# A gated-MLP stage in nine chunks of 512 tokens, with matmul operands set apart in SBUF

## The chip, the cores and the metric

The kernel runs on one core of a Trainium2 chip. The metric is device time in microseconds (us) for one execution. The kernel before takes 1077.67 us, the median of three runs (1074.98, 1077.67, 1080.53). A core has a matmul engine (TensorE, PE in the profile; its weight loads are PEld), VectorE (DVE), ScalarE (ACT), GpSimd (POOL) and SyncE (SP), which here issues nearly all DMAs. Each engine runs its own queue in order. Data lies in SBUF, 128 partitions wide; a "word" below is 4 bytes of one partition, and "columns" is the free size of a matmul's moving operand.

## The reference

Attention with positive random features, then a gated MLP over the 4608 tokens:

```python
def phi(x):                       # x scaled by D**-0.25
    h = x @ omega.T - sum(x*x)/2
    return exp(h - max(h)) / sqrt(128)
kv  = einsum('bhsm,bhsd->bhmd', phi(k), v)
z   = phi(k).sum(axis=2)
num = einsum('bhsm,bhmd->bhsd', phi(q), kv)
den = einsum('bhsm,bhm->bhs', phi(q), z)[..., None] + 1e-06
x   = (num / den) as (4608 tokens, 512)          # 8 batches x 576 tokens, 8 heads x 64
out = (sigmoid(x @ w_gate) * (x @ w_val)) @ w_out   # 512 -> 1536 -> 512
```

All arithmetic is float32. The matmuls of the MLP are made of parts: an operand a is split into a high part (rounded to fp32r, the type that TensorE takes at full speed) and a low part a - high, and a product is the sum of three matmuls, low x high, high x low and high x high.

## The kernel before, in words

**Stage 1** (to 457.77 us) computes the attention and, between its matmuls, the gate and value products of the first NE = 4 of the 12 column tiles of the hidden layer (`products`, L534, output `gv`), in chunks of 512 tokens of which the first is two of 256. Its order comes from a planner, `Turns`, that simulates the engines with costs written in the code. The attention's output goes to DRAM as `xT`, and stage 1's gated values as `ye`. From 390.65 us on only the products are left. At the end of stage 1 `first_operands` loads and divides the operands of stage 2's first chunk, and `early_unit` (L459) loads and divides the first UL = 5 weight units that `late_weights` had stored in `w32`. A unit is the seven sums and blocks of a weight matrix that Strassen's scheme wants, in a high and a low part.

**Stage 2** (`second_pass` L692, `gated` L618, matmuls at L634, output `gw`) does the other 8 column tiles, as four pairs of tiles, with Winograd's form of Strassen's 2 x 2 scheme: seven products instead of eight. Tokens go in NCW = 6 chunks of 768; the two halves of a chunk (W = 384 tokens) are one dimension of the 2 x 2 scheme, so a matmul has 384 columns. In each chunk a loop runs over the four pairs, and for each over kind 0 (gate) and kind 1 (value): eight groups, n = 0 to 7. A group has 7 products of 6 matmuls: 42. A group's matmuls and its evacuations on ACT, DVE and POOL stand in an order written by hand (`pin` keeps it): products 1, 6, 5, then the previous group's last two (4, 3; "held", so 12 matmuls of a group run within the next one), then 2 and 7. Between them `between` runs the work that a plan names for (chunk, group, place): loading and dividing the next chunk's operands (`operands`, L585), in chunk 0 the division of the UE = 3 units that stage 1 has not divided (twelve steps, three to a group from group 1), and in the last chunk the first loads of stage 3 (`first_values`, L767). DVE adds the products up from PSUM (`add`, L616); after kind 1 POOL does seven steps for the pair, and the seven combinations that stage 3 wants go to DRAM as `yl`, in two parts, `ya` (4 of 7) and `yb` (3 of 7). `put` (L687) issues these stores on SP, at the next group of kind 1.

The stage-2 operands xh and xl (high and low part of one of seven combinations) lie in one buffer of a ring of 8 (`buffer`, L435): XL = 7 in the pool `late`, XE = 1 in the pool `tail`. Each is [2, 2, W] words, 6144 bytes in a partition. Six more units, those of the output weights, come into the units' places in the last chunk (`unit`, L440; the DMA is L445): one after each of the groups 1 to 5, the last behind the loop.

**Stage 3** (`last(g)`, L787, matmuls at L810, output `po`) goes over 18 groups of 2 x 128 tokens. For each of six slices j it takes the seven combinations (`gated_values`, L731: for j below 2 from `ye`, with four sums at L752, else from `yl`), divides them into yh and yl (`parts_of`, L754: ACT at L760, then DVE or POOL at L762) and runs 21 matmuls of 256 columns; here yh or yl is the loaded weight, and the unit is the moving operand. yh and yl lie in the same ring of buffers, at an offset in words: APART = 80, but where PLACED names (g, j) its pair of offsets. The values of the groups' slices j >= 2 lie in one tile for a group: group 0's tile takes a unit's place. After slice 0 of group 0, the loads of group 1 are issued; after slice 1, the last stores of stage 2.

The places in SBUF follow from the pools: `const` has a pad, `below`, of 80 words. In the kernel before, stage 2's units and operand buffers all begin at the same place modulo 512 bytes.

## Time and the profile before

| | |
|---|---|
| median of three runs | 1077.67 us |
| the profiled execution | 1078.5 us |
| its span | 1076.7 us |
| instructions | 26339 |
| TensorE matmul busy | 1050.9 us, 98%, 10556 |
| DVE, ACT, POOL busy | 758.3, 491.5, 404.3 us |
| DMA moved | 226.32 MB |
| stage 2's matmuls (L634) | 2016 of 384 columns, 334 ns each |
| stage 3's matmuls (L810) | 2268 of 256 columns, 280 ns each |

The span is the time from the first to the last instruction in the trace. The ns of a matmul is its own duration; matmuls are pipelined and overlap, so the distance from one start to the next, the pace, is shorter, and the share of busy time says little. What sets the time is read from the chain of waits (what each step waited for, followed back from the end) and from counts in windows.

### The profile page before, as it was taken

The page shows a single profiled execution, that of the slowest core. Times are in us where ns is not written, and L with a number is a line of the kernel's source. Part 1 is how long each engine was busy: PE and PEld are TensorE (multiplying, and loading weights), DVE is VectorE, ACT ScalarE, POOL GpSimd, SP SyncE. Part 2 cuts the span into 40 slices and gives each one's busy share as a digit, 9 for nine tenths or more (in the row PEclk, how much of TensorE's full clock was granted, in tenths as well). Part 3 has the DMA queues.
Part 4 walks back from the last instruction along what each step waited for, and adds up shares of the span by engine and source line. Part 5 has one row for each costly group of instructions (what it writes and reads, how often), then busy time and mean ns, then how long its engine had stood idle before and what let it go on. Part 6 is the DMA issues. An engine that isn't in the chain of part 4 may idle for free.

```text
span 1076.7 us, 26339 instructions
## 1 busy us (share of the span) xinstructions
PE 1050.9 (98%) x10556; PEld 979.2 (91%) x10556; DVE 758.3 (70%) x1482; ACT 491.5 (46%) x1026; POOL 404.3 (38%) x326
## 2 busy tenths in 40 slices
PE   6789999999999999999999999999999999999998
PEld 5678888878788888899999999999999999999998
DVE  3999989999889954457747574756658666666663
ACT  6687676675555554333323232323223444443342
POOL 0331513432524323026756676656544111111111
PEclk9889999999999999999999999999999999999999
DMA  7587979898886666152423324242798765555661
GB/s 283 182 288 245 311 273 376 254 371 282 276 272 234 233 241 240 49 213 78 146 103 132 133 78 165 74 162 103 245 397 287 238 213 185 194 188 202 206 216 40
DMA packets 121322, 226.32 MB, mean 210 GB/s; under 512 B 10992, under 2 KB 59888, under 8 KB 118128
## 3 DMA queue, kind: packets, MB, share of 16 engines
q1 hardware_dynamic: 115872, 215.39, 57.8%
q10 hardware_dynamic: 5328, 9.24, 2.3%
q8 instruction: 83, 1.36, 0.5%
q14 instruction: 39, 0.32, 0.1%
HBM read 144.90 MB, written 79.69 MB: 209 GB/s over the span
## 4 chain that ended last, share of the span: by engine, by line
PE 94%; DMA 2%; DVE 2%; ACT 1%; issue 0%; SPq 0%; DVEq 0%; ACTq 0%
PE gw L634 33%; PE po L810 24%; PE gv L534 18%; PE ppq L932 4%; PE ppk L932 3%; PE pnq L1079 3%; PE pkv L1014 3%; PE ptq L1062 3%; PE pxq L1104 2%; DMA xT<-xsq 1%; ACT kpk L990 1%; DMA c8r<-w 0%; DMA rawk<-kT 0%; DVE sqq L879 0%; DMA natq<-qn 0%
## 5 line engine op out<-in xcount | busy, mean ns | idle before, releaser
L634 PE MATMUL gw<-xl,u 128*128 128x384 f32 x2016 | 350.5, 334 | 0.0
L634 PEld LDWEIGHTS gw<-xl,u 128*128 128x128 f32 x2016 | 349.2, 188 | 1.0 <-issue 0.9
L810 PE MATMUL po<-u,yh 128*128 128x256 f32 x1512 | 264.3, 280 | 0.0
L810 PEld LDWEIGHTS po<-u,yh 128*128 128x128 f32 x1512 | 230.0, 188 | 0.0
L810 PE MATMUL po<-u,yl 128*128 128x256 f32 x756 | 211.5, 280 | 0.0
L534 PE MATMUL gv<-xe,wh 128*128 128x512 f32 (+1 forms) x640 | 189.7, 376 | 0.0
L760 ACT ACTIVATE yh<-yr 128x896 fp32r<-128x896 f32 x108 | 102.5, 954 | 152.3 <-PE po L810 67.6
L762 DVE TENSOR_TENSOR yl<-yr,yh 128x896 fp32r<-128x896 f32 x91 | 102.4, 1129 | 63.3 <-ACT yh L760 62.9
L810 PEld LDWEIGHTS po<-u,yl 128*128 128x128 f32 x756 | 143.8, 190 | 0.2 <-DVE yl L762 0.2
L534 PEld LDWEIGHTS gv<-xe,wh 128*128 128x128 f32 x640 | 115.3, 189 | 19.5 <-issue 0.5
L534 PE MATMUL gv<-xe,wl 128*128 128x512 f32 (+1 forms) x320 | 120.7, 377 | 0.0
L762 POOL TENSOR_TENSOR yl<-yr,yh 128x896 fp32r<-128x896 f32 x17 | 37.0, 2177 | 208.9 <-ACT yh L760 184.0
L616 DVE TENSOR_TENSOR u<-gw,p 128x384 f32<-128x384 f32 x96 | 53.3, 555 | 67.1 <-PE gw L634 45.8
L683 POOL TENSOR_TENSOR ya<-ya,g 128x384 f32<-128x384 f32 x48 | 59.9, 1249 | 96.5 <-issue 36.7
L642 ACT ACTIVATE g<-g 128x384 f32<-128x384 f32 x72 | 37.8, 526 | 108.9 <-DVE g L616 108.8
L510 POOL TENSOR_TENSOR xe<-xr,xe 128x512 fp32r<-128x512 f32 (+1 forms) x40 | 49.5, 1261 | 80.1 <-ACT xe L501 80.1
L990 ACT ACTIVATE kpk<-ppk,nbk 128x128 f32<-128x128 f32 x256 | 70.9, 393 | 8.3 <-DVE nbk L948 8.2
L534 PEld LDWEIGHTS gv<-xe,wl 128*128 128x128 f32 x320 | 60.6, 189 | 9.9 <-PE pxq L1104 0.4
L939 DVE TENSOR_REDUCE sqk<-ppk 128x8 f32<-128x1024 f32 (+1 forms) x48 | 45.1, 953 | 20.9 <-PE ppk L932 20.7
L1067 ACT ACTIVATE qpq<-ptq 128x512 f32<-128x512 f32 (+1 forms) x80 | 42.1, 563 | 36.4 <-PE ptq L1062 36.1
L939 DVE TENSOR_REDUCE sqq<-ppq 128x8 f32<-128x1024 f32 (+1 forms) x48 | 45.5, 955 | 11.2 <-PE ppq L932 10.9
L752 DVE TENSOR_TENSOR yr<-yr 128x128 f32<-128x128 f32 x144 | 40.1, 322 | 18.7 <-DMA yr<-ye 18.2
(227 smaller groups left out, 1560.5 us busy)
## 6 DMA issues: line engine op xcount, KB each, us to landing
yr<-yl SPq DMA_DIRECT2D x72, 448.0 KB, 5.1
yl<-ya SPq DMA_DIRECT2D x24, 768.0 KB, 3.5
yl<-yb SPq DMA_DIRECT2D x24, 576.0 KB, 4.4
u<-w_parts SPq DMA_DIRECT2D x6, 1792.0 KB, 10.7
v<-va SPq DMA_DIRECT2D x32, 330.0 KB, 5.5
out<-o ACTq DMA_DIRECT2D x34, 256.0 KB, 5.5
natq<-qn SPq DMA_DIRECT2D x32, 256.0 KB, 5.5
xT<-xsq SPq DMA_DIRECT2D x64, 128.0 KB, 2.9
```

What stands on the lines that cost most here:

```text
L510: nc.gpsimd.tensor_tensor(out=x[:, 1], in0=raw[:, k], in1=x[:, 0].bitcast(F32), op=ALU.subtract)
L534: nc.tensor.matmul(gv, lhsT=u[:, s], rhs=v, start=(m == 0), stop=(m == 3 * KC - 1))
L616: return nc.vector.tensor_tensor(out=o, in0=a, in1=b, op=ALU.add)
L634: nc.tensor.matmul(o, lhsT=u[:, k, s], rhs=v[:, kc, :], start=(first and m == 0), stop=(m == 5), skip_group_check=not first,)
L683: pin(nc.gpsimd.tensor_tensor(out=o, in0=a, in1=b, op=op))
L760: pin(nc.scalar.activation(out=yh, in_=x, func=AF.Copy))
L762: pin(engine.tensor_tensor(out=yl_, in0=x, in1=yh.bitcast(F32), op=ALU.subtract))
L810: nc.tensor.matmul(o, lhsT=u[:, i, :], rhs=v[:, k, :], start=(j + m == 0 and n in (1, 6, 5, 3)), stop=(j == NPAIR - 1 and m == 2), skip_gr ...
L932: nc.tensor.matmul(pp[r, h, k, :], lhsT=raw[HALVES[h], o + r.start : o + r.stop], rhs=om_sb[HALVES[h], :], start=True, stop=True,)
L939: nc.vector.tensor_reduce(out=z[:, :, :, 0], in_=pp, axis=AX.X, op=ALU.max)
L990: nc.scalar.activation(out=kp[t][:, h, :], in_=pp[:, h, i, :], func=AF.Exp, bias=nb[:, h, i : i + 1],)
L1067: nc.scalar.activation(out=qp, in_=pt, func=AF.Exp)
```

## The change

- W is 2 x 128, so stage 2 has NCW = 9 chunks of 512 tokens, matmuls of 256 columns, 72 groups; `yl`, the stores and all tiles of a chunk shrink with it.
- The ring of operand buffers has 10 places (7 in `late`, 3 in `tail`) of ROOM = 1152 words (4608 bytes). Pads of 80 words (above the operands in `late`) and 48 words (below them in `tail`) are allocated. In stage 2 the two parts stand at words 0 and 512 of the buffer, but for operands 0, 4, 3 of chunks 1 and 4 (MIXED) at 624 and 96.
- In stage 3 the offset APART is 32, and PLACED is (48, 64) for slices (0, 1), (1, 0), (4, 0) and (10, 0).
- Stage 1 divides six units (UL = 6), the sixth behind the last chunk's inputs; stage 2's chunk 0 divides two (eight steps).
- The plan for the next chunk's operands spreads over the groups 2 to 7 and has nothing left in the next chunk's group 0.
- All six late units go into `late`'s places, after the groups 1 to 6 of the last chunk.
- Group 0's values in stage 3 get a tile of their own ("yr").

```diff
-W = 3 * P
+W = 2 * P
...
-XL, XE = 7, 1
-UL, UE = 5, 3
-PLACED = {(0, 1): (0, 48), (2, 0): (0, 48), (4, 0): (80, 0), (6, 0): (96, 112), (8, 0): (12, 10), (10, 0): (0, 48)}
-BELOW, APART = 80, 80
+XL, XE = 7, 3
+UL, UE = 6, 2
+BELOW, ABOVE_X, BELOW_X = 80, 80, 48
+ROOM, APART = 1152, 32
+MIXED = {(c, n) for c in (1, 4) for n in (0, 4, 3)}
+PLACED = dict.fromkeys(((0, 1), (1, 0), (4, 0), (10, 0)), (48, 64))
...
     def buffer(name):
         at, n = (late, XL) if turn_of[0] % (XL + XE) < XL else (tail, XE)
         turn_of[0] += 1
-        return at.tile([P, 2, 2, W], F32R, tag="x", bufs=n, name=name)
+        if turn_of[0] == XL + 1:
+            tail.tile([P, BELOW_X], F32, name="below_x")
+        return at.tile([P, ROOM], F32R, tag="x", bufs=n, name=name)
+
+    def operand(c, n):
+        b = buffer(f"xl{c}_{n}")
+        return [b[:, o : o + 2 * W].rearrange("p (k t) -> p k t", k=2) for o in ((624, 96) if (c, n) in MIXED else (0, 2 * W))]
...
     def early_unit(n):
         t = yield from after(stored[n], 0)
+        if n == UL - 1:
+            t = yield from after(x_ready[-2][-1], t)
...
     def high(x, n, a, c):
-        b = buffer(f"xl{c}_{n}")
-        x[n] = b[:, 0], b[:, 1]
-        pin(nc.scalar.activation(out=b[:, 0], in_=a, func=AF.Copy))
+        x[n] = operand(c, n)
+        pin(nc.scalar.activation(out=x[n][0], in_=a, func=AF.Copy))
...
             (c - 1, 2, 2): [combined(s, a21, a22, ALU.add)],
-            (c - 1, 3, 2): [combined(a21, a11, a21, ALU.subtract)],
-            (c - 1, 4, 2): [parts(0, a11, nc.gpsimd)],
-            (c - 1, 5, 2): [combined(a11, s, a11, ALU.subtract)],
-            (c - 1, 7, 0): [parts(4, a11, nc.vector)],
-            (c - 1, 7, 1): [parts(3, s, nc.gpsimd)],
-            (c - 1, 7, 2): [
-                parts(1, a12, nc.vector), parts(5, a21, nc.gpsimd), combined(a12, a12, a11, ALU.subtract),
-            ],
-            (c, 0, 1): [parts(2, a22, nc.vector), parts(6, a12, nc.vector)],
+            (c - 1, 3, 0): [combined(a21, a11, a21, ALU.subtract)],
+            (c - 1, 3, 2): [parts(0, a11, nc.gpsimd)],
+            (c - 1, 4, 0): [combined(a11, s, a11, ALU.subtract)],
+            (c - 1, 4, 2): [parts(1, a12, nc.vector)],
+            (c - 1, 5, 1): [parts(4, a11, nc.vector)],
+            (c - 1, 6, 0): [combined(a12, a12, a11, ALU.subtract)],
+            (c - 1, 7, 0): [parts(3, s, nc.gpsimd)],
+            (c - 1, 7, 1): [parts(2, a22, nc.vector)],
+            (c - 1, 7, 2): [parts(6, a12, nc.vector), parts(5, a21, nc.gpsimd)],
...
-                    if c == NCW - 1 and 1 <= n <= UL:
+                    if c == NCW - 1 and 1 <= n <= NPAIR:
                         unit(late, UL + UE + n - 1)
-            if c == NCW - 1:
-                unit(tail, N_LATE - 1)
...
             if len(groups) == g:
+                t, n = ("u", UE) if g else ("yr", 1)
                 groups.append(
-                    tail.tile([P, NPAIR - EP, N_OPS, P], F32, tag="u", bufs=UE, name=f"yr{g}") if g < 2 else groups[g - 2]
+                    tail.tile([P, NPAIR - EP, N_OPS, P], F32, tag=t, bufs=n, name=f"yr{g}") if g < 2 else groups[g - 2]
                 )
...
-            buffer(f"{t}{g}_{j}").rearrange("p a b t -> p (a b t)")[:, at : at + N_OPS * P].rearrange("p (o t) -> p o t", t=P)
+            buffer(f"{t}{g}_{j}")[:, at : at + N_OPS * P].rearrange("p (o t) -> p o t", t=P)
...
                 for n in (0, 4, 3, 1, 5, 2, 6):
-                    b = buffer(f"xl0_{n}")
-                    x[n] = b[:, 0], b[:, 1]
+                    x[n] = operand(0, n)
+                late.tile([P, ABOVE_X], F32, name="above_x")
```

## The prediction

> **What bounds the kernel now.** I read the page first, then the chain of waits, then windows of the matmul lines, then the queues around the change from stage 2 to stage 3.
>
> ```profile
> span 1076.7 us, 26339 instructions
> PE 1050.9 (98%) x10556; PEld 979.2 (91%) x10556; DVE 758.3 (70%) x1482; ACT 491.5 (46%) x1026; POOL 404.3 (38%) x326
> ...
> 390.65 67.12 PE gv L534 x296
> 457.77 348.09 PE gw L634 x2004
> 805.86 2.48 PE po L810 x21
> 808.34 2.08 PE gw L634 x12
> 810.42 260.57 PE po L810 x2235
> ```
>
> TensorE is busy for 98% of the span, and from 390.65 the chain is TensorE alone. So a time is a number of matmuls by a pace (start to start), plus the places where TensorE waits. Stage 2 (L634) takes 348.09 + 2.08 = 350.17 us, stage 3 (L810) 2.48 + 260.57 = 263.05 us. The profiled execution took 1078.5 us: the span and 1.8 us around it. The median of the three runs is 0.8 us lower, so I sum against 1078.5 and take 0.8 off.
>
> Paces come from windows: a window holds the matmuls that touch it, so the pace is the window plus one matmul's duration over the count. A row has the window and its length, then busy time and (count) of TensorE and of its weight loads, the granted clock, the DMA engines' busy share and their GB/s; the first two rows are of the costliest groups and end in the mean ns of one.
>
> ```profile
> L634 PE MATMUL gw<-xl,u 128*128 128x384 f32 x2016 | 350.5, 334 | 0.0
> L810 PE MATMUL po<-u,yh 128*128 128x256 f32 x1512 | 264.3, 280 | 0.0
> ...
> 470.00:740.00 270.00, 270.00 (x1556) 269.31 (x1556) 1.00 0.34 121
> ...
> 838.00:895.00 57.00, 57.00 (x487) 57.00 (x486) 1.00 0.62 204
> 896.20:898.60 2.40, 2.40 (x23) 2.40 (x22) 1.00 0.93 311
> 926.00:953.00 27.00, 27.00 (x240) 27.00 (x239) 1.00 0.61 205
> 970.00:1060.00 90.00, 90.00 (x767) 90.00 (x766) 1.00 0.54 183
> ...
> 120.20:123.40 3.20, 3.20 (x29) 3.20 (x28) 1.00 1.04 383
> ```
>
> The fourth line is the 384-wide matmul of stage 2: (270.00 + 0.334)/1556 = 173.7 ns, the whole stage at one pace. The next four are the 256-wide matmul of stage 3, which has **two paces**: (57.00 + 0.28)/487 = 117.6 and (90.00 + 0.28)/767 = 117.7 ns in the first and last, (27.00 + 0.28)/240 = 113.7 ns in the third. The granted clock is 1.00 in all of them, so it is not the clock. The kernel spreads stage 3's operands by an offset per group and slice (PLACED, APART): each change of pace that I found stands at a PLACED entry, and the pace then stays. The 2.40 us window is the block of (6, 0), with offsets 96 and 112; it runs at (2.40 + 0.28)/23 = 116.5 ns, and behind it the groups are fast. The last line is a 256-wide matmul of stage 1, whose buffers all begin at the same place modulo 512 bytes as its weights: (3.20 + 0.28)/29 = 120.0 ns. Same shape, three paces: the operands' places look like the cause. I take 113.5 ns for the fast pace (113.7, less half a matmul's edge of the count) and 117.7 for the slow one.
>
> **The change part by part.** *Stage 2's matmuls.* They go from 2016 of 384 columns to 9 x 8 x 42 = 3024 of 256. By the diff's sizes I place the new buffers: the pads of 80 and 48 words put the stage-2 operands at 80 words modulo 128 from their weights, and the MIXED ones at 96 and 112; in stage 3 the smaller APART of 32 on a base of 48 gives 80 again, and (48, 64) gives 96 and 112. So both stages have stage 3's usual distance and, at marked blocks, the mixture that came before its fast groups. Chunk 0, with no mixture ahead of it, I take as slow: 336 x 117.7 ns = 39.55 us. Chunks 1 and 4 hold three mixed operands: 144 x 116.5 + 192 x 113.5 ns = 38.57 us each. The other six: 6 x 336 x 113.5 ns = 228.8 us. The sum is 345.5 us against 350.17: **-4.7 us**. The fast pace has never been seen with L634, so this is the least certain term; its bounds are all slow, 3024 x 117.7 ns = 355.9 (+5.7), or 120.0 ns, 362.9 (+12.7), above and all fast, 343.2 (-7.0), below. I stay near the fast end because the distances are those of stage 3.
>
> The Trainium skill ("TensorE: Matmul & The Clock Gate", section "Back-to-back issue gap") gives N/2.4 + 2.5 ns for an isolated warm matmul. That is 109.2 ns at 256 and 162.5 at 384, so by it the stage would become 3024 x 109.2 - 2016 x 162.5 ns = 2.6 us longer: a price per matmul that speaks against narrower ones. The trace has 173.7 ns at 384, 11 ns over the rule, and 113.7 at 256, 4.5 over it; so the rule's price is not this kernel's, and I give it no chance of its own.
>
> *Stage 3's matmuls.* Their number stays: 18 x 126 = 2268. The mixture at (0, 1), (1, 0), (4, 0) and (10, 0) should keep all of it fast: 84 x 116.5 + 2184 x 113.5 ns = 257.7 us against 263.05: **-5.4 us** (-5.6 to +3.9, the latter for 117.7 throughout).
>
> *Loads at the change of stage.* Six 1792 KB units are loaded within the last chunk, which shrinks from 336 x 173.7 ns = 58.4 us to 38.1.
>
> ```profile
> 766.50:819.80 53.30, 53.30 (x345) 53.30 (x344) 34.29 (x51) 13.72 (x23) 31.19 (x27) 1.00 0.99 371
> 780.00:787.00 7.00, 7.00 (x43) 7.00 (x42) 2.88 (x6) 1.40 (x3) 3.65 (x4) 1.00 1.04 434
> ...
> 760.01 0.36 SPq L690 DMA_DIRECT2D yl<-ya  x1
> ...
> 761.57 4.82 SPq L745 DMA_DIRECT2D yr<-ye  x6
> 766.49 1.55 SPq L445 DMA_DIRECT2D u<-w_parts  x2
> ...
> 796.53 1.76 SPq L747 DMA_DIRECT2D yr<-yl  x4
> ...
> 803.81 0.33 SPq L445 DMA_DIRECT2D u<-w_parts  x1
> 804.23 5.49 SPq L745 DMA_DIRECT2D yr<-ye  x6
> ...
> 817.47 3.25 DVE L752 TENSOR_TENSOR yr<-yr 128x128 f32<-128x128 f32 x7
> ...
> yl<-ya SPq DMA_DIRECT2D x24, 768.0 KB, 3.5
> yl<-yb SPq DMA_DIRECT2D x24, 576.0 KB, 4.4
> u<-w_parts SPq DMA_DIRECT2D x6, 1792.0 KB, 10.7
> yr<-yl SPq DMA_DIRECT2D x72, 448.0 KB, 5.1
> ...
> L760 ACT ACTIVATE yh<-yr 128x896 fp32r<-128x896 f32 x108 | 102.5, 954 | 152.3 <-PE po L810 67.6
> L762 DVE TENSOR_TENSOR yl<-yr,yh 128x896 fp32r<-128x896 f32 x91 | 102.4, 1129 | 63.3 <-ACT yh L760 62.9
> L752 DVE TENSOR_TENSOR yr<-yr 128x128 f32<-128x128 f32 x144 | 40.1, 322 | 18.7 <-DMA yr<-ye 18.2
> ...
> PEld po L810 <- DVE yl L762: 0.2, 1, 0.2
> ```
>
> The first two rows are windows again, with DVE, ACT and POOL ahead of the last three columns; then come timelines (start, length, what was issued or run, its count) and DMA issues (KB each). From the first unit's issue at 766.49 the DMA engines are 99% busy, at 371 GB/s (434 in the best 7 us), until 819.80. Behind the six units, on the same queue, come group 1's first values (issue at 804.23), and TensorE met its first block of them just in time: 0.2 us. Bytes from the first unit's issue to those values, each row's KB by 1024: six units 11.0 MB, three pairs' stores 4.1, group 0's other values 1.8, group 1's first slice (4 blocks of 128 x 128 values, 256 KB) 0.3, together 17.2 MB, or 46.4 us: 812.9. Four sums, an ACT copy and a subtraction follow; the sums began at 817.47, 4.5 us behind that estimate, with TensorE due at 810.42 + 105 x 0.114 = 822.4. After the change the stores are 896 KB a pair, and it is 15.9 MB, or 42.7 us (36.6 at 434 GB/s). Before, the last pair's store came 12.5 us into the chunk, which starts at 457.77 + 1668 x 0.1737 = 747.5, and the unit 6.5 us later. The store goes with the chunk's length, 12.5 x 38.1/58.4 = 8.2; the issues behind it keep their 6.5. So the values land at 8.2 + 6.5 + 42.7 = 57.4 us after the chunk's start, and TensorE could use them 4 x 0.322 + 0.954 + 1.129 = 3.4 us later, at 60.8. It is due at 38.1 + 12 x 0.1135 + 126 x 0.1135 = 53.8. That is a wait of **+7.0 us**, which did not exist before: 0.8 at 434 GB/s, 11.5 with the 4.5 us that the estimate was early. I take the middle, the rate of the whole stretch. That the sixth unit's load is now in the loop and yr0 has a place of its own takes a wait off SP, but the bytes ahead of group 1 stay, so neither gains here.
>
> *Division, seams, the rest.*
>
> ```profile
> L616 DVE TENSOR_TENSOR u<-gw,p 128x384 f32<-128x384 f32 x96 | 53.3, 555 | 67.1 <-PE gw L634 45.8
> L616 DVE TENSOR_TENSOR u2o<-po,p1o 128x256 f32<-128x256 f32 x18 | 7.5, 419 | 8.8 <-PE po L810 8.8
> L454 DVE TENSOR_TENSOR u<-u 128x512 fp32r<-128x512 f32 x9 | 7.3, 814 | 2.7 <-ACT u L453 2.7
> L683 POOL TENSOR_TENSOR ya<-ya,g 128x384 f32<-128x384 f32 x48 | 59.9, 1249 | 96.5 <-issue 36.7
> L407 POOL TENSOR_TENSOR c7r<-c,c7r 128x256 f32<-128x256 f32 x2 | 1.5, 738 | 0.1
> ...
>   issue: 0.9, 5
> ```
>
> An evacuation on DVE falls from 555 to 419 ns, but there are 72 groups instead of 48. A group lasts 42 x 0.1135 = 4.77 us and has 5.5 of them, 2.3 us: free, as now. In chunk 0 eight halved units are divided at three to a group: 3 x 0.814 + 5.5 x 0.419 = 4.75 us of DVE in 4.77. That has no slack, so I charge **+1.0 us**, between 0 and 3.6 (three groups late by one division and one evacuation, 1.2 each). POOL's seven steps a pair go from about 7 x 1.2 = 8.4 us to about 7 x 0.74 = 5.2, in a pair of 9.5 us: free. TensorE had 0.9 us of hiccups at five chunk changes; eight make 1.4: **+0.5 us** (0 to 2, should DVE be short there). The sixth unit divided in stage 1 waits on SP for the last chunk's inputs and adds two ACT and two DVE steps beside 67 us of dense matmuls: nothing.
>
> **Sum:** -4.7 - 5.4 + 7.0 + 1.0 + 0.5 = -1.6, so 1076.9 us for a profiled execution and **1076.1 us** for the median.
>
> **The rivals.** *B, the loads come in time.* If DMA holds its best rate through the seam and DVE keeps up, no term but the two paces is left: 1077.7 - 10.1 = 1067.6 us. For it: 434 GB/s is in the trace, and fewer bytes of stores compete. Against: the mean over 53 us is 371, with the same transfers.
>
> *C, the mixture does not hold.* The pace could fall back at a second mixture: (2, 0) and (10, 0) in the present stage 3 turned fast groups slow, though with other offsets. With chunks 5 to 8 and six groups of stage 3 slow: 4 x 336 x 4.2 ns = 5.6 us and 6 x 126 x 4.2 ns = 3.2 us more, and 1.2 us less wait as the last chunk is longer: 1083.7 us.
>
> *D, slower: the pace never turns fast.* The mechanism is a fixed price per matmul, at place or by the way the weights come in, that no pad removes, or the change not giving the distances that I worked out. All of both stages at 117.7 ns: stage 2 +5.7, stage 3 +3.9, the wait 5.3 (TensorE is due later), 1.5 for the rest: 1077.7 + 16.4 = 1094.1 us; with stage 2 at 120.0 ns some 6 us more. It decides from the point at which stage 2's mean pace passes 115.8 ns (350.17/3024). For it: 384 columns need 173.7 ns, 0.452 a column, and 0.452 x 256 = 115.8 leaves nothing for a fixed part, while the 256-wide matmuls of the stage-1 window and of two thirds of stage 3 run at 117.6 or more. Against: 27 us at 113.7 directly behind the very mixture that is now used.
>
> The Trainium skill ("TensorE: Matmul & The Clock Gate", section "Step-by-step: what each phase is for") says that weights and moving operand have read ports of their own and a weight load takes nothing from the running matmul. By it a distance between the two buffers would buy nothing, and D would follow. The trace disagrees so far as it goes: one instruction on one shape at 113.7 and at 117.7 ns.
>
> **How the numbers follow.** Forecast 0.45, B 0.28, C 0.13, D 0.14. A measurement of this kernel can tell about 0.5%, 5.4 us, from no change: 1072.3 and 1083.1 are the bounds. The forecast's own range is 1069.9 (wait of 0.8) to 1083.2 (wait 11.5, division 3.6): 0.14 of it faster, 0.28 the same, 0.03 slower. B is faster. C lies at the upper bound, 0.06 the same and 0.07 slower; D is slower. Together 0.42, 0.34, 0.24. The range reaches from 1066, B with a little to spare, to 1085, C with the same, and leaves out D and the tails.
>
> **What would show it.** Count L634 in a window of chunks 5 to 8: 113 to 114 ns right, 117 or more C or D; the same for L810 in groups 12 to 17. In the chain, a gap ahead of L810 about 15 us into stage 3, released by L762 or L760, which in turn waited for values from ye; none there is B. On SP, the first w_parts issue should stand 14 to 16 us into the last chunk. DVE waits in groups 1 to 3 of chunk 0 should show the division. I am wrong outright if TensorE waits by more than 3 us in chunks 1 to 7, or if the pace changes at blocks that are not marked.

## The result, and the profile after

The changed kernel takes 1093.84 us, the median of four runs (1093.35 to 1094.26), beside 1078.32 for the kernel before in the same session: a ratio of 1.0144, 95% interval 1.0125 to 1.0164. It is slower by 1.4%. The forecast was 1076.1 us, with a range up to 1085.

First the page of the profile after, and its chain of waits (start, length, what it was spent on, count):

```profile
span 1091.6 us, 28952 instructions
PE 1049.0 (96%) x11564; PEld 974.7 (89%) x11564; DVE 780.6 (72%) x1636; ACT 498.7 (46%) x1117; POOL 407.6 (37%) x419
...
813.38 11.90 DMA yr<-ye
...
831.45 108.89 PE po L819 x943
...
944.07 2.11 POOL yl L771
946.23 12.21 PE po L819 x105
960.30 2.33 DVE yl L771
963.86 2.11 DMA yr<-ye
...
971.62 1.09 DVE o L626 x3
974.64 2.13 POOL yl L771
```

TensorE is busy for 1.9 us less than before, but the span is 14.9 us longer. The chain before was TensorE alone from 390.65 us on; now it leaves TensorE around the change of stage (mostly for DMA, 781 to 831) and from 941 on again and again, for DVE, the loads of first values, the evacuations with their stores, and POOL.

The windows of the two matmul lines (columns as in the prediction):

```profile
500.00:539.00 39.00, 39.00 (x339) 39.00 (x338) 1.00 0.34 121
579.00:606.00 27.00, 27.00 (x241) 27.00 (x240) 1.00 0.41 142
607.60:616.00 8.40, 8.40 (x74) 8.40 (x73) 1.00 0.27 96
655.00:769.00 114.00, 114.00 (x1008) 114.00 (x1008) 1.00 0.35 124
...
861.00:918.00 57.00, 57.00 (x504) 57.00 (x504) 1.00 0.56 194
1010.00:1086.00 76.00, 72.43 (x628) 71.44 (x627) 1.00 0.46 160
```

Stage 2 runs at (39.00 + 0.28)/339 = 115.9 ns in chunk 1, which holds mixed operands, and at (114.00 + 0.28)/1008 = 113.4 in chunks 5 to 7; stage 3 at 113.7 in groups 2 to 5. The second and third rows are chunk 3, where nothing is marked: (27.00 + 0.28)/241 = 113.2 ns up to 606 us, (8.40 + 0.28)/74 = 117.3 behind 607.6. In the last row a window of 76 us holds 628 matmuls, 121.5 ns each: there TensorE waits.

From the starts of all matmuls in the two traces I made the sums below: the time at the pace, and as waits what a distance from start to start has above the pace, where it is over 135 ns (200 at 384 columns).

| us | before | after |
|---|---|---|
| first matmul of stage 2 to the last of stage 3 | 614.5 | 629.5 |
| of it at the pace | 613.7 | 603.7 |
| waits in chunk 0 | 0.05 | 4.3 |
| waits in the chunks between | 0.5 | 0.4 |
| waits from the last chunk's start to group 2 | 0.3 | 10.8 |
| waits in groups 2 to 7 | 0.0 | 0.0 |
| waits in groups 8 to 17 | 0.0 | 10.3 |

So the paces gave 10.0 us, as forecast (about 4 in stage 2 and 6 in stage 3), and three waits took 25.

**The waits of groups 8 to 17.** The lists of what matmuls and weight loads of L819 waited for say who ends them (both engines count, so a wait stands here nearly twice):

```profile
  POOL yl L771: 15.4, 18
```

All of it lies in groups 8 to 17; DVE's yl, next in the list, is named for 1.3 us there. POOL makes yl of a group's last slice only. Why is it late? These rows of four timelines, put in order of time, are one turn of it, around the start of group 8 at 933.3 (a row joins neighbouring instructions; in brackets the idle time before and what ended it):

```profile
927.31 4.49 ACT L769 ACTIVATE yh<-yr 128x896 fp32r<-128x896 f32 x5 [7.35 <-DVE yl L771]
928.40 2.13 POOL L771 TENSOR_TENSOR yl<-yr,yh 128x896 fp32r<-128x896 f32 x1 [13.19 <-ACT yh L769]
929.14 3.34 DVE L771 TENSOR_TENSOR yl<-yr,yh 128x896 fp32r<-128x896 f32 x2 [2.26 <-ACT yh L769]
931.50 3.40 SPq L754 DMA_DIRECT2D yr<-ye  x6
931.71 0.36 ACT L835 ACTIVATE p1o<-po 128x256 f32<-128x256 f32 x1
933.28 0.95 ACT L769 ACTIVATE yh<-yr 128x896 fp32r<-128x896 f32 x1 [1.21 <-issue]
934.85 0.70 DVE L761 TENSOR_TENSOR yr<-yr 128x128 f32<-128x128 f32 x3 [2.37 <-DMA yr<-ye]
...
938.71 0.42 DVE L626 TENSOR_TENSOR u2o<-po,p1o 128x256 f32<-128x256 f32 x1
...
941.14 1.72 ACTq L846 DMA_DIRECT2D out<-o  x2
942.99 4.32 ACT L769 ACTIVATE yh<-yr 128x896 fp32r<-128x896 f32 x5 [8.76 <-DMA out<-o]
944.07 2.10 POOL L771 TENSOR_TENSOR yl<-yr,yh 128x896 fp32r<-128x896 f32 x1 [13.55 <-ACT yh L769]
```

ACT makes five yh in a row: the last slice of group 7 and four of group 8. DVE makes two yl from them; the first of them frees a place for first values, and only then SP issues the loads of group 9's (931.50). DVE's next instructions are group 9's sums, which wait for those loads (2.37 us), and the evacuation of group 7 stands behind them: it begins at 938.71, 5.4 us after the group's last matmul. ACT's next instructions are a copy out of PSUM (931.71), one more yh (933.28) and the stores of that evacuation; the yh of group 8's last slice stands behind the stores: 942.99, 15.68 us after the one of group 7. POOL needs 2.1 us for its yl, and TensorE, which reached that slice at 933.3 + 105 x 0.1133 = 945.2, starts it at 946.23. The loop ACT, DVE, SP, DVE, ACT takes about 15.5 us a group; TensorE's 126 matmuls take 14.28.

In the kernel before, around the start of its group 9 at 939.2 (fast there too):

```profile
937.75 0.70 DVE L752 TENSOR_TENSOR yr<-yr 128x128 f32<-128x128 f32 x3 [1.22 <-DMA yr<-ye]
...
939.36 0.42 DVE L616 TENSOR_TENSOR u2o<-po,p1o 128x256 f32<-128x256 f32 x1
...
941.93 0.82 ACTq L837 DMA_DIRECT2D out<-o  x2
942.88 2.04 ACT L760 ACTIVATE yh<-yr 128x896 fp32r<-128x896 f32 x2 [2.66 <-DVE o L616]
...
945.05 2.12 POOL L762 TENSOR_TENSOR yl<-yr,yh 128x896 fp32r<-128x896 f32 x1 [12.17 <-DVE yl L762]
```

The evacuation begins 0.1 us after the group's last matmul, as only a part of the sums stands ahead of it, and POOL ends at 947.2, 4 us before TensorE comes to the last slice. Stage 3 is not pinned behind group 0: its order on ACT and DVE is generated when the kernel is built, from the places that are free. In both kernels ACT has five yh between a group's stores and its next copy out of PSUM. But with ten places instead of eight they run one slice further ahead: the yh of a group's last slice, which POOL needs, is the first of the five instead of the second (POOL starts behind it, at 944.07 and 945.05). On DVE, all eight sums of group 9 now stand ahead of the evacuation of group 7; in the kernel before, some sums stand between the evacuation's steps.

**The waits at the change of stage.**

```profile
781.00:826.00 45.00, 42.22 (x352) 41.83 (x351) 23.83 (x47) 12.07 (x24) 17.61 (x24) 0.96 0.97 369
...
785.73 0.37 SPq L700 DMA_DIRECT2D yl<-yb  x1
...
797.82 0.74 POOL L693 TENSOR_TENSOR yb<-g,ya 128x256 f32<-128x256 f32 x1 [6.50 <-DMA yl<-yb]
799.27 0.42 DVE L626 TENSOR_TENSOR g<-gw,p 128x256 f32<-128x256 f32 x1 [5.09 <-POOL yb L693]
...
813.38 9.52 SPq L754 DMA_DIRECT2D yr<-ye  x6
...
827.47 2.34 DVE L761 TENSOR_TENSOR yr<-yr 128x128 f32<-128x128 f32 x7
```

The DMA engines are 97% busy for 45 us, at 369 GB/s. A store of yb, issued at 785.73 behind two units, keeps its one place until 797.8: POOL waits 6.50 us for it, DVE 5.09 us for POOL, and TensorE 2.4 us at 801 (by the starts of the matmuls). POOL waits in the same way at 808.6, 4.58 us. Group 1's first values, issued from 813.38 on, land from 825.28 (813.38 + 11.90 in the chain) to 826.13, 56.7 us after the chunk's start at 769.4. DVE comes to their sums at 827.47, behind evacuations of group 0, and TensorE takes them up at 831.45, after 4.2 us of waiting. The rest of the 10.8 us is in small waits behind these two and in group 0.

**The waits of chunk 0.**

```profile
460.62 0.86 SPq L457 DMA_DIRECT2D u<-w  x2
465.29 0.63 ACT L462 ACTIVATE u<-u 128x512 fp32r<-128x512 f32 x1 [2.37 <-DMA u<-w]
...
469.26 0.42 DVE L626 TENSOR_TENSOR u<-gw,p 128x256 f32<-128x256 f32 x1
```

The first unit is issued at 460.62; ACT waits 2.37 us for it, with its first division step ahead of other work, and DVE, whose own step follows ACT's, comes to the evacuation of group 2's first products at 469.26, where TensorE loses 1.9 us. DVE has no pause then until 475; one of its steps, at 472.20, takes 1.18 us beside POOL instead of 0.7. These waits differ from one execution to the next: the same code of chunk 0 had 3.7 to 6.8 us of them in the kernels below.

### The profile page after: what moved, and what is told of

Same layout as the page of the kernel before. It is cut to its first block, busy times and chain, and to the rows that moved or that the text cites. A ratio compares the mean times of both kernels' runs of the same rounds, so it can differ in the third digit from the quotient of the medians.

```text
span 1091.6 us, 28952 instructions
## 1 busy us (share of the span) xinstructions
PE 1049.0 (96%) x11564; PEld 974.7 (89%) x11564; DVE 780.6 (72%) x1636; ACT 498.7 (46%) x1117; POOL 407.6 (37%) x419
## 4 chain that ended last, share of the span: by engine, by line
PE 81%; DMA 6%; DVE 5%; ACT 2%; issue 2%; POOL 1%; SPq 1%; ACTq 0%; DVEq 0%; POOLq 0%
PE gw L644 27%; PE gv L545 19%; PE po L819 16%; PE pkv L1023 4%; PE pnq L1088 3%; PE ppk L941 3%; PE ppq L941 3%; PE ptq L1071 3%; PE pxq L1113 2%; DMA yr<-ye 2%; DVE yl L771 1%; DMA u<-w_parts 1%; POOL yl L771 1%; DMA yl<-yb 1%; ACT yh L769 1%
## 5 line engine op out<-in xcount | busy, mean ns | idle before, releaser
L644 PE MATMUL gw<-xl,u 128*128 128x256 f32 x3024 | 349.3, 278 | 5.5 <-DVE u L626 5.3
L644 PEld LDWEIGHTS gw<-xl,u 128*128 128x128 f32 x3024 | 348.0, 189 | 6.8 <-DVE u L626 6.1
L819 PE MATMUL po<-u,yh 128*128 128x256 f32 x1512 | 260.4, 278 | 0.0
L819 PEld LDWEIGHTS po<-u,yh 128*128 128x128 f32 x1512 | 229.5, 189 | 0.0
L819 PE MATMUL po<-u,yl 128*128 128x256 f32 x756 | 211.4, 280 | 11.9 <-POOL yl L771 6.8
L769 ACT ACTIVATE yh<-yr 128x896 fp32r<-128x896 f32 x108 | 97.5, 946 | 158.2 <-PE po L819 58.1
L819 PEld LDWEIGHTS po<-u,yl 128*128 128x128 f32 x756 | 142.7, 189 | 14.4 <-POOL yl L771 8.6
L771 DVE TENSOR_TENSOR yl<-yr,yh 128x896 fp32r<-128x896 f32 x91 | 115.0, 1282 | 32.5 <-ACT yh L769 32.2
L626 DVE TENSOR_TENSOR u<-gw,p 128x256 f32<-128x256 f32 x144 | 60.5, 420 | 57.5 <-PE gw L644 42.5
L652 ACT ACTIVATE g<-g 128x256 f32<-128x256 f32 x108 | 44.6, 419 | 112.1 <-DVE g L626 111.9
L693 POOL TENSOR_TENSOR ya<-ya,g 128x256 f32<-128x256 f32 x72 | 57.0, 792 | 83.1 <-issue 39.6
L667 ACT ACTIVATE g<-gw 128x256 f32<-128x256 f32 x36 | 13.8, 385 | 104.3 <-PE gw L644 79.0
```

Of the source, the lines that this page charges most:

```text
L626: return nc.vector.tensor_tensor(out=o, in0=a, in1=b, op=ALU.add)
L644: nc.tensor.matmul(o, lhsT=u[:, k, s], rhs=v[:, kc, :], start=(first and m == 0), stop=(m == 5), skip_group_check=not first,)
L652: pin(nc.scalar.activation(out=g[i], in_=g[i], func=AF.Sigmoid))
L693: pin(nc.gpsimd.tensor_tensor(out=o, in0=a, in1=b, op=op))
L769: pin(nc.scalar.activation(out=yh, in_=x, func=AF.Copy))
L771: pin(engine.tensor_tensor(out=yl_, in0=x, in1=yh.bitcast(F32), op=ALU.subtract))
```

## The experiments

All times of the kernel before in these sessions lie between 1073.5 and 1080.3 us. "A" is the changed kernel, "B" the one before. Two theories of the loop stood against each other: that the ring of ten places makes it (ring), and that any kernel has it whose groups take less than 15 us (speed).

**A with eight places and the old plan of operands** (`a_ring8`). The plan in `operands` is that of the kernel before, line for line.

```diff
-XL, XE = 7, 3
+XL, XE = 7, 1
...
```

> The changed kernel with the operand ring of the kernel before: 8 places instead of 10, and the old plan for the next chunk's operands, which 8 places need. Theory R (ring): with ten places the generated order of stage 3 puts yh one slice further ahead, and the evacuation of a group, its stores on ACT, the next yh and the next loads close a loop of about 15.5 us a group, longer than TensorE's 14.28. With 8 places the order is the old one again, groups 8 to 16 take 14.3 us each, stage 3 is 10 to 12 us shorter, and the kernel takes about 1083 us, or up to 1086 if the old plan costs TensorE some waits at the chunks' seams. Theory S (speed): the loop is as long with any ring and only shows because the groups became faster than 15 us; then the groups stay at 15 us or more and the time stays within 2 us of 1094.

Measured: 1090.19 us, ratio 1.0117 (1.0096 to 1.0139).

```profile
986.50:1070.00 83.50, 83.50 (x739) 83.50 (x738) 1.00 0.62 202
```
Groups 11 to 16 run at (83.5 + 0.28)/739 = 113.4 ns and groups 2 to 17 have no wait at all: the loop is gone, for the ring theory. The total misses the expected 1083 to 1086: the old plan costs 6.4 us of waits in chunks 1 to 7 (among them L644 behind POOL's xl), and chunks 5 to 7 ran at 117.5 ns, behind the mixture of chunk 4. So the new plan, and the ten places that it needs, save 6 us of waits in stage 2.

**B with the change's offsets in stage 3** (`b_fast3`)

```diff
-PLACED = {(0, 1): (0, 48), (2, 0): (0, 48), ...}
+PLACED = dict.fromkeys(((0, 1), (1, 0), (4, 0), (10, 0)), (96, 112))
```

> The kernel before with nothing changed but the offsets of stage 3: (96, 112) at slices (0,1), (1,0), (4,0) and (10,0), 80 elsewhere, so that its distances are those of the changed kernel's stage 3. Pace theory: L810 runs at 113.3 ns throughout instead of 117.8 in twelve groups. Theory R (ring): with 8 places nothing else becomes late, each group takes 14.3 us, and the kernel takes 5.5 us less, about 1072.8. Theory S (speed): the same waits as in the changed kernel appear once groups take 14.28 us, the gain is eaten, and it takes 1078 or more.

Measured: 1072.83 us (median of ten), ratio 0.9964 (0.9930 to 0.9998): seven runs from 1066.9 to 1073.4, three from 1081.0 to 1082.1.

```profile
920.00:1060.00 140.00, 140.00 (x1236) 140.00 (x1236) 1.00 0.57 187
```

(140 + 0.28)/1236 = 113.5 ns, and no wait in groups 2 to 17, sixteen groups of 14.3 us each. The speed theory falls: with eight places nothing is late at this speed. It is the one kernel here whose median lies below both, by 0.4%, in runs that spread over 15 us. Only the run of 1069.08 us has a trace; that the three long ones had the slow pace is inferred from their times.

**A with three places for first values** (`a_xr3`), in `gated_values` and in `operands`, which share them.

```diff
-tag="xr", bufs=2
+tag="xr", bufs=3
```

> The changed kernel with three places instead of two for the first values of stage 3 (and for stage 2's inputs, which share them). Loop theory: the loop of 15.5 us a group goes through the loads of the values ye, which wait until DVE has used the group's before; with a third place the loads are issued before that, DVE's sums wait less, the evacuation comes earlier, and most of the 10 us of waits in groups 8 to 16 goes: about 1084 to 1087. Rival: ACT and POOL alone, the stores behind the evacuation and the 2.1 us of POOL for the last slice, hold the loop; then the waits stay and the time is within 2 us of 1094.

Measured: 1083.07 us (1080.48 to 1092.67), ratio 1.0069 (1.0034 to 1.0104).

```profile
933.00:1070.00 137.00, 137.00 (x1210) 137.00 (x1210) 1.00 0.54 184
```

The waits of groups 8 to 17 are 0.0 us, (137 + 0.28)/1210 = 113.5 ns. The ring and the order of ACT and SP are those of the changed kernel. DVE's generated order is not: with the third place a group's sums come behind the first yl after the evacuation and behind the third, instead of behind the third and the fourth. So the loop needs the link from the first values to DVE, but whether the earlier loads or DVE's new order opens it is not separated. The medians differ by 10.8 us, near the size of the waits, in part by chance: in the traced run chunk 0 waits 2.5 us more than in the changed kernel.

**A with two places for yb** (`a_yb2`), in stage 2 and for stage 3's outputs.

```diff
-tag="yb", bufs=1
+tag="yb", bufs=2
```

> The changed kernel with two places for yb instead of one (and for stage 3's outputs, which share the place). Theory: in the last chunk POOL waits for the store of the last yb, which stands behind two units' loads in the DMA queue (6.5 us at 791), DVE waits for POOL, and TensorE waits 2.4 us at 801. With two places that wait goes, and the time is about 2.5 us less. Rival: the transfers, not the places, are what is late; TensorE meets group 1's first values as late as before, the 2.4 us go over into the 4.2 us ahead of group 1, and the time stays within 1 us.

Measured: 1089.63 us (1086.92 to 1096.46), ratio 1.0124 (1.0084 to 1.0163).

```profile
796.98 18.46 DMA yr<-yl
```

POOL no longer waits for yb's place (its step at 792.37 starts with no wait), and TensorE's 2.4 us in the last chunk are gone. But the chain then waits 18 us for group 0's values and TensorE 4.0 us at 817.65 and 5.0 at 834.62; the waits from the last chunk to group 2 are 14.1 us in this profile. The rival holds for the mechanism: group 0's values are issued 26.6 us after the last chunk's start (770.38) instead of 33.1, but the first of them lands after 45.1 us, and after 45.0 in the changed kernel. The transfers are late, not the place. The runs spread too far for a verdict on the time.

**A without the last chunk's stores** (`a_nostore`)

```diff
-        stores.extend(((to[:, :, :4], ya), (to[:, :, 4:], yb)))
+        if c < NCW - 1:
+            stores.extend(((to[:, :, :4], ya), (to[:, :, 4:], yb)))
...
-            pin(nc.sync.dma_start(out=raw[:, :N_OPS], in_=yl[j - EP, :, g]))
+            pin(nc.sync.dma_start(out=raw[:, :N_OPS], in_=yl[j - EP, :, min(g, (NCW - 1) * SUB - 1)]))
```

The last two groups load a block of the chunk before in the place of their own, so the loads stay and the kernel leaves out the output of the last 512 tokens.

> The changed kernel without the last chunk's stores of yl (four pairs of 896 KB, 3.7 MB); the groups 16 and 17, which would read them, read group 15's or 16's block of the chunk before, so that the output of the last 512 tokens is left out, and the same loads are made. Bytes theory of the 11 us around the change of stage: three of the stores, 2.75 MB or 7.4 us at 371 GB/s, stand ahead of group 1's first values, and POOL waits for the fourth's place; without them TensorE's waits between the last chunk's start and group 2 fall from 10.8 to about 3 to 4 us. Issue theory: it is the order of the issues on SP and the chain behind the loads that counts, not the bytes; then 8 us or more of waits stay. The loop of stage 3 is not touched; its 10 us stay, or begin a little later.

Measured: 1085.88 us (one run).

```profile
812.68 11.82 PE po L820 x103
825.20 1.08 DVE o L626 x3
827.33 64.69 PE po L820 x567
```

From the last chunk to group 2 only 0.4 us of waits are left of 10.8. The chain stays on TensorE but for one evacuation at 825. So it is the stores. The waits fall by 10.4 us, more than the 7.4 us that the bytes take at the mean rate; how much of it is bytes and how much the places that the stores hold is not separated here. The loop stays, 9.6 us, and begins in group 6 already: a stage that starts without delay has less in hand.

**A with the division two steps to a group, from group 1** (`a_div`)

```diff
-{(0, 1 + i // 3, i % 3): [do] ...
+{(0, 1 + i // 2, 2 * (i % 2)): [do] ...
```

> The changed kernel with the eight division steps of chunk 0 spread two to a group over the groups 1 to 4, ahead of and behind the group, instead of three to a group. Theory: TensorE's 4.3 us of waits in chunk 0 come from DVE's queue, which is full there (three steps of about 0.7 and 5.5 evacuations of 0.42 and the next chunk's sums in 4.8 us); spread, less than 2 us of them are left, and the time is 2 to 3 us less. Rival: the first step waits for its unit's load (ACT 2.4 us at 465) and holds the queue behind it wherever it stands; then at most 1 us is gained.

Measured: 1087.69 us (1086.78 to 1092.68), ratio 1.0106 (1.0076 to 1.0135). But chunk 0's waits are 4.25 us, as before. The time came from elsewhere: groups 1 to 3 stood in the slow pace, and the loop began to hold TensorE only in group 14 (2.2 us instead of 10.3). The theory that spreading the steps helps is not borne out, as far as one trace can tell.

**A with three places for first values and the division from group 2** (`a_best`)

```diff
+tag="xr", bufs=3
-{(0, 1 + i // 3, i % 3): [do] ...
+{(0, 2 + i // 2, 2 * (i % 2)): [do] ...
```

> The changed kernel with three places for stage 3's first values, and with the eight division steps of chunk 0 at two to a group over the groups 2 to 5 instead of three to a group from group 1. Load theory of chunk 0: the first step's ACT copy waits 2.4 us for its unit (issued at 460.6, landed at 465.3) and holds ACT's and then DVE's queue, so that steps from group 2 on, at about 467, wait for nothing; the 4 to 7 us of waits in chunk 0 fall below 2. Queue theory: DVE is simply full in chunk 0, and spread steps leave the waits as they are (4.3 us with the steps in groups 1 to 4). By the first about 1079 to 1080, by the second 1083. In neither does it beat the kernel before, since the 11 us around the change of stage stay.

Measured: 1081.34 us, ratio 1.0050 (1.0028 to 1.0073). Chunk 0's first wait fell from 1.9 to 0.4 us, but later ones of 0.6 to 1.1 us took its place, where division and the next chunk's sums meet: 3.5 us in all. Neither theory's number came out, and what each has is open, since the same code of chunk 0 had 3.7 to 6.8 us of waits in different kernels here. As expected it does not beat the kernel before.

**What the pace hangs on.** Five kernels.

`b_384fast`: B with the change's pads, distances and offsets, 768-token chunks kept; the mixture goes to the one operand of a chunk whose place has room for it.

```diff
-BELOW, APART = 80, 80
+BELOW, ABOVE_X, BELOW_X = 80, 80, 48
+ROOM, APART = 1536, 32
+MIXED = {(1, 0), (2, 4), (3, 3), (4, 1), (5, 5)}
```

> The kernel before, chunks of 768 and everything else kept, with the change's distances alone: pads of 80 and 48 words, so that stage 2's operands stand 80 words from their weights instead of 0, 96 and 112 for the one operand of a chunk that lies in the tail place (chunks 1 to 5; five of 35 operands there), and in stage 3 the change's offsets. Theory P (places): the distance is what a matmul's pace hangs on at any width, and the fast pace saves the same 6.7 ns on a matmul of 384 columns (113.3 ns and 128 columns more at 0.417 ns: 166.7 against 173.3); stage 2 becomes 336.1 us, 13 us less, stage 3 5.5 us less, and the kernel takes about 1060 us, or about 1069 if the matmuls of 384 only reach the slow one of the two paces (171.1 ns). Theory N (narrow): 384 columns run at their own pace whatever the places, since it needs 0.452 ns a column like the fast pace at 256; stage 2 stays, and the time is that of the stage-3 offsets alone, about 1073.

Measured: 1078.29 us (1069.37 to 1083.91), ratio 1.0009 (0.9975 to 1.0043).

```profile
456.00:512.00 56.00, 56.00 (x319) 56.00 (x319) 1.00 0.41 153
514.00:740.00 226.00, 226.00 (x1301) 225.36 (x1300) 1.00 0.34 120
```

176.6 ns in chunk 0 and (226 + 0.33)/1301 = 174.0 from chunk 1 on: no gain over 173.7 at distance 0. Theory N holds for stage 2: the places alone give it nothing at 384 columns. They gave something only with the narrower matmul. The median lies 5 us over N's 1073, in runs that spread over 14 us.

`a_flat`: A with every matmul at 80 words.

```diff
-MIXED = {(c, n) for c in (1, 4) for n in (0, 4, 3)}
-PLACED = dict.fromkeys(((0, 1), (1, 0), (4, 0), (10, 0)), (48, 64))
+MIXED = set()
+PLACED = {}
```

> The changed kernel without the mixtures: every matmul of stage 2 and 3 at the distance of 80 words. If the mixtures are what turns the pace fast, L644 runs at 117.8 ns throughout: stage 2 takes 356 us and some 4 of waits, 10 us more than the changed kernel; in stage 3, groups of 14.8 us leave less of the loop's 15.5 to be seen, so it loses only 4 to 6 us more: about 1105. If the pace goes by chance and not by the mixtures, it takes any value between 1090 and 1105 and the paces change inside the stages.

Measured: 1095.5 us (one run).

```profile
503.00:580.00 77.00, 77.00 (x656) 77.00 (x655) 1.00 0.34 119
659.00:768.00 109.00, 109.00 (x962) 108.86 (x961) 1.00 0.35 123
...
852.00:1086.00 234.00, 234.00 (x1989) 234.00 (x1988) 1.00 0.54 186
```

Stage 2 runs at 117.8 ns in chunks 1 and 2 and at (109 + 0.28)/962 = 113.6 later, without any mixture; stage 3 at 117.8 throughout, and there the groups have no waits. So a mixture is not needed to turn the pace, and the expectation of a slow stage 2 missed. With slow groups of 14.84 us the loop is not met at all: groups 2 to 17 take 237.3 us, 1.9 less than in the changed kernel with its shorter groups and their waits, where 4 to 6 more were expected. A turn of the loop is shorter while TensorE does not wait: in the changed kernel the stores of three early groups begin at 865.45, 880.33 and 895.01 us, 14.9 and 14.7 apart. Groups of 14.28 us lose about half a microsecond a group on that until, in group 8, nothing is left in hand.

`a_zero`: `a_flat` with stage 2 at distance 0.

```diff
-BELOW, ABOVE_X, BELOW_X = 80, 80, 48
-ROOM, APART = 1152, 32
+BELOW, ABOVE_X, BELOW_X = 80, 128, 128
+ROOM, APART = 1152, 80
```

> The changed kernel with stage 2 at distance 0, as in the kernel before, and stage 3 at 80 without mixtures. If distance 0 gives what the 256-wide matmuls of stage 1 show, L644 runs at 120 ns: 363 us of matmuls, 17 us more than the changed kernel in stage 2, about 1110 to 1115 in all. If distance 0 is no worse than 80 without mixtures, L644 runs at 117.8 and the time is that of the kernel without mixtures.

Measured: 1101.96 us (one run).

```profile
500.00:780.00 280.00, 280.00 (x2336) 280.00 (x2335) 1.00 0.33 118
```

(280 + 0.28)/2336 = 120.0 ns, in every chunk. The change's distances are worth (120.0 - 114.3) x 3024 = 17 us in stage 2 (114.3 ns is its mean pace in the changed kernel without the waits), against narrow matmuls at the old place. The total is lower than expected since stage 3 ran fast here, mostly.

`b_flat80` and `b_48`: B with `PLACED = {}` and 80 or 48 words in all of stage 3; and `b_map`, another distance in each group.

```diff
-PLACED = {(0, 1): (0, 48), (2, 0): (0, 48), ...}
+PLACED = {}
...
-BELOW, APART = 80, 80
+BELOW, APART = 80, 48
...
+MAP = (80, 0, 64, 8, 96, 16, 72, 24, 112, 32, 88, 40, 104, 48, 120, 56, 80, 4)
+PLACED = {(g, j): (d, d) for g, d in enumerate(MAP) for j in range(6)}
```

> The kernel before with one distance of 80 words in all of stage 3 and no mixture. If the mixtures set the pace, no mixture leaves the slow pace of 117.8 ns for the 18 groups wherever the stage begins slow: times lie in one narrow cluster, about 1081 if slow, about 1067 if fast. If the state is taken by chance as the stage begins, the times of several executions form two clusters, about 1067 and 1081.

> The kernel before with one distance of 48 words in all of stage 3 and no mixture; in the map that was the distance whose group ran at 113.4 ns between groups at 117 to 120. If 48 words give the fast pace by themselves, L810 runs at 113.3 ns from the first group to the last in every execution, and the times lie close together at about 1067, 11 us below the kernel before. If two states are possible at 48 words as at 80, the times form two clusters, about 1067 and 1081, or one at 1081.

> The kernel before with another distance in every group of stage 3, in all its slices: 80, 0, 64, 8, 96, 16, 72, 24, 112, 32, 88, 40, 104, 48, 120, 56, 80, 4 words for the groups 0 to 17. If the pace hangs on the distance alone, each group has a pace of its own, 120.0 ns at 0 and 113.3 at the best; if there are only two states that stay until something turns them, the groups show 113.3 or 117.8 whatever the distance, and 120.0 near 0.

Measured: b_flat80 1081.29 us (1078.27 to 1082.91), ratio 1.0055 (1.0034 to 1.0077); b_48 1079.73 us (1076.39 to 1083.19), ratio 1.0022 (1.0002 to 1.0041); b_map 1076.26 us (one run).

```profile
822.00:1070.00 248.00, 248.00 (x2108) 248.00 (x2108) 1.00 0.58 190
```
```profile
817.60:832.50 14.90, 14.90 (x126) 14.90 (x125) 1.00 0.71 221
997.20:1011.30 14.10, 14.10 (x127) 14.10 (x126) 1.00 0.63 201
1040.90:1055.00 14.10, 14.10 (x127) 14.10 (x126) 1.00 0.49 167
```

At 80 words without mixture, the first row, (248 + 0.28)/2108 = 117.8 ns over all of stage 3; the row of 48 words is the same to the digit. In the map, distance 0 gives (14.90 + 0.28)/126 = 120.5, 48 words 113.2 and, three groups later, 80 words 113.2 (each window is short, so half a matmul is 0.5 ns). So 48 words, fast in the map, are slow when they stand alone: the distance does not set one pace, and the hope for a kernel that is always fast fell. Nor is 120 ns kept for distance 0: the map's groups at 64, 40 and 104 words run at 120.0 too, the first of them right behind the group at 0.

**What stands where the pace turns.** In the changed kernel the pace of chunk 3 turned slow at 607 us, at two distances between starts of 163 and 225 ns, a wait of 0.16 us. In stage 3 of `a_zero`, which has no mixture, it turned slow at 1017.4 and fast at 1048.0 us; in `a_yb2` it turned at 981.6, 996.7, 1011.3 and 1026.6, slow and fast by turns. Each of these six stands at one of the loop's waits of TensorE, 0.1 to 1.0 us long. Most waits do not turn it: the changed kernel with a third place for first values has the same short wait at 606.7 us and is fast again four matmuls later. So a short wait can turn the pace as a mixed block can; why one does and another does not is open.

## Why the prediction was wrong, point by point

- **Stage 2's matmuls, -4.7 us, and stage 3's, -5.4.** Right in size: the time at the pace fell by 10.0 us, 10.1 were forecast, and most of it ran at 113.3 ns. In mechanism right only in part, and so in part by luck. That the distance makes the matmul faster than 120.0 ns was borne out. That a marked block turns the pace and that it then stays was not: it turned slow at 607 us in chunk 3, at a block that is not marked, which the prediction gave as a sign that it is wrong outright; `a_flat` turned fast without any mixture, and `a_ring8` was slow behind one.
- **Stage 3: the step that failed.** The sum took stage 3 as 2268 matmuls by a pace, with no wait behind group 1, and did not cost the ring's two more places at all: the change from one tail place to three was never asked what it does to the order of work in stage 3. It measured 10.3 us in groups 8 to 17. The row from which the step was made, fast groups without waits in the kernel before, came from another order, with the ring of eight. The run with eight places has no such wait at the same speed, nor has the one with a third place for first values. The measured time lies 17.7 us over the forecast: 10.3 are this step, 3.8 and 3.3 the two waits that follow.
- **Loads at the change of stage, +7.0 us.** The right mechanism, mis-sized: 10.8. The values were forecast to land 57.4 us after the chunk's start and landed at 56.7, but TensorE took them up at 62.0 instead of 60.8, since DVE came to their sums only after evacuations of group 0. What was left out is the one place of yb, which let the queue stop POOL, DVE and TensorE within the last chunk, and the small waits behind both. In the kernel before, too, the values had landed by 815.29, and it was DVE, with four yl in 6.61 us from 810.93, that began the sums at 817.47; so about half of the 4.5 us that the prediction put on the loads was DVE's. The 11.5 us at the other end of that term held it.
- **Division, +1.0 us.** Mis-sized: 4.3, over the bound of 3.6. The forecast counted DVE's work (4.75 of 4.77 us) and not the load that the first step waits for, nor DVE's steps beside POOL; which of these made the waits is open, as neither run on it settled it.
- **Seams, +0.5 us.** Wrong in sign, and small: 0.4 us in chunks 1 to 7 against 0.5 before.
- **The rivals.** The time is that of rival D, 1094.1 us, and by chance: D had all matmuls at 117.7 ns, and they ran at 114. The point from which D was to decide, a mean pace of stage 2 over 115.8 ns without waits, was not reached. B and C did not come about.
- **Ports.** The kernel at distance 0 ran at 120.0 ns for 2336 matmuls and the changed one at 113.4 to 115.9 with the same instruction. By the Trainium skill ("TensorE: Matmul & The Clock Gate", section "Step-by-step: what each phase is for") weights and moving operand have read ports of their own, and by that alone the distance would not matter; the measurement differs, and decides. In the loop, two yl on DVE, 1.08 us each elsewhere, took 3.34 us together at 929.14 while POOL ran from 928.40 to 930.53. The Trainium skill ("SBUF — State Buffer", section "SBUF: two separate sides") says that GpSimd and a DVE instruction with two SBUF inputs share a port pair, which the one that starts first holds for its whole instruction. The trace agrees with that.

## What to carry to other kernels

A buffer count is a term of the sum: where the order of instructions is generated, more places can move work ahead of the work that somebody waits for, and the loop over engines has to be added up for one period and held against the bounding engine's. Three waits of 4 to 11 us ate a gain of 10 us that came out in size, and none shows in a share of busy time. When a stage becomes shorter, count the bytes that must pass at its end, and count every single place that a store holds on the way.

## What the runs showed of the hardware

- A 128 x 256 matmul of fp32r parts has one pace, 120.0 ns, when moving operand and weights begin at the same place modulo 512 bytes (2336 matmuls of `a_zero`); in `b_map` it had it at 40, 64 and 104 words as well. At 80 words it has two, 113.3 and 117.8 ns, which stay for hundreds of matmuls; at 48 words both were seen as well. With mixed blocks the fast one seems more frequent (seven of ten runs of `b_fast3` lie at 1066.9 to 1073.4 us, none of six of `b_flat80` below 1078.2 and none of ten of `b_48` below 1076.3), but it turns without them too, in the traces here at short waits of TensorE. What decides whether it turns is not settled.
- A 384-wide matmul gained nothing from the same distance: 174.0 ns at 80 words, 173.7 at 0, and 176.6 through one whole chunk. A pace measured at one width did not carry to another by a fixed cost and a slope.
- The changed kernel's four runs lie within 1 us (1093.4 to 1094.3); `a_yb2`, which has the loop too, spreads over 9.5 us (1086.9 to 1096.5). So the loop alone does not make the times steady.
